# A third token tile among the first: tile 2 loaded earlier, transposed raw, and centred by a matmul

## The chip, the cores and the metric

The kernel runs on one core of a Trainium2 chip. The time is device microseconds (us) of one execution, as the median of several; a profiled execution gives the trace from which all durations here come. The engines are TensorE (PE; PEld is its weight load), VectorE (DVE), ScalarE (ACT), GpSimd (POOL) and SyncE (SP). SyncE, ScalarE and GpSimd each also issue DMAs on a queue of their own. On-chip memory is SBUF; matmuls write to PSUM, which has eight banks of 512 float32 columns by 128 partitions.

## The reference

The input x has 2048 tokens of 512 features, in bfloat16. Tokens are normalised (layer norm without weights), and two branches are added to x:

```
xn = (x - mean(x)) / sqrt(var(x) + 1e-5)
# branch A: a diagonal complex recurrence over the tokens
Lam_bar = exp(dt * Lam);  Bu = xn @ B_bar.T
h[t] = Lam_bar * h[t-1] + Bu[t]
A = 2 * real(h @ C.T) + xn * Dskip
# branch B: a gated feed-forward layer, F = 1376
B = (silu(xn @ w_gate) * (xn @ w_up)) @ w_down
out = x + A + B
```

## The kernel before, in words

The 2048 tokens are handled in four chunks of 512, each made of four tiles of 128 tokens. Tokens arrive with a token per partition, but a matmul that contracts over the 512 features needs features on partitions, so each tile has to be transposed. For chunks 1 to 3 this is done by a transposing DMA after the norm (`xT_dma`, L262). Chunk 0 would have to wait too long for that, so its first three tiles are treated differently; this is the part that the change touches.

The order of each engine's instructions is the order of the program text: the scheduler is switched off (`manual_schedule`, L64). Each engine executes its own list in order and waits by semaphores for what it reads and for the buffers that it overwrites. VectorE's work for later stages is held in a list, `backlog`, from which `pump` emits pieces between TensorE's matmuls (L623 to L649).

**Loads.** The first DMAs are listed at L125 to L143. On SyncE's queue: tile 0 of x, the first half (feature rows k = 0, 1) of the first gate group, tile 2 of x, both halves of the first up group, tile 3, then the other weights and chunk 1. On ScalarE's queue: tile 1, and the second half (k = 2, 3) of the first gate group. The weights of the gate and up matrices come in three groups of columns: two of 512 and one of 352.

**Chunk 0, tiles 0 and 1.** `raw_mm` transposes the raw tile by four matmuls against an identity (L238), each giving a 128x128 block k in PSUM. The mean is taken off inside PSUM: `sum_dve` (L221) lets VectorE sum a tile's features, and `cT_mean` (L245) adds, by a matmul of that sum, broadcast, against a matrix of -1/512 on the diagonal, the negative mean to the blocks. `raw_copy` (L249) copies the blocks to `xcT`, alternating between ScalarE and VectorE. The division by the deviation is not applied to the tokens; it is applied as the `scale` of the activation that evicts each result (`sw_scale`, L495).

**Chunk 0, tile 2** is centred by VectorE: `center` (L225) sums the tile, scales the sum to a mean, and subtracts it. Four matmuls transpose the centred tile into one bank, and ScalarE copies it out in one piece (L730 and L731).

**Chunk 0, tile 3** goes through the norm on VectorE and a transposing DMA (`xT0_dma`, L258). Tiles 0 to 2 are normalised on VectorE as well, for branch A.

**Head of the matmul stream.** `head_mm` (L693) multiplies a tile, as stationary operand, by rows of the first gate or up group, and `held` keeps a PSUM bank for each tile and matrix. Gate for tiles 0 and 1 comes first, row by row, then up rows 0 and 1, tile 2's transposes, up rows 2 and 3, then gate and up of tile 2. `sw_out` (L508) evicts a pair on ScalarE: Silu of the gate to `g0`, and a scaled copy of the up result; a product on VectorE follows. The loop at L779 does the other column groups and tile 3.

**Statistics.** `ln_stats` (L183) and `ln_stats_half` (L187) are VectorE's mean and variance; `ln_rstd` (L192) adds the epsilon on VectorE and takes the power -1/2 on GpSimd. ScalarE's evictions of a tile wait for its rstd. GpSimd also computes `dt_t`, an exponential of the parameters (`exp_pool`, L282), which arrive by `prm_transpose` (L277).

**Afterwards** come the B projections (`bproj_tile`, L380) of chunk 0, the rest of the gate/up work, and then, chunk after chunk, projections, gate/up, and the output matmuls (L599 with w_down, L612 with the recurrence's result). SyncE's queue carries the transposing DMAs in program order: chunk 0's, B's two, chunk 1's, the gate-up product of chunk 0 (`g0_dma`, L525, in two calls), then w_down, C's two, chunk 1's last gate-up block and chunk 2's tokens.

Of the kernel before, what the change touches and what calls it, by code (L numbers as in the profile page):

```python
# [10 lines left out]
F32 = mybir.dt.float32  # L11
BF16 = mybir.dt.bfloat16
ALU = mybir.AluOpType
# [10 lines left out]
def kernel(  # L24
# [17 lines left out]
    nc = tc.nc  # L42
    _, L, D = A_x.shape
# [4 lines left out]
    HW = CW // 2  # L48
# [3 lines left out]
    KD = D // 128  # L52
# [11 lines left out]
    const = ctx.enter_context(tc.tile_pool(name="const", bufs=1))  # L64
# [9 lines left out]
    def bank(shape=(128, CW), dtype=F32):  # L74
        return psum.tile(list(shape), dtype, name="ps")
# [4 lines left out]
    x_v = A_x[0].rearrange("(n p) d -> p n d", p=128)  # L80
# [5 lines left out]
    xall = const.tile([128, NT, D], BF16, name="xall")  # L86
# [30 lines left out]
    def load_w1_half(q, tiles, view, gi, k0, k1):  # L117
        a, b = fgroups[gi]
        q.dma_start(out=tiles[gi][:, k0:k1, :], in_=view[:, k0:k1, a * 128:min(F, b * 128)])

    HK = KD // 2
# [4 lines left out]
    nc.vector.memset(xall[:, 1, 0:2], 0.0)  # L126
    nc.scalar.dma_start(out=xall[:, 1, :], in_=x_v[:, 1, :])
    nc.scalar.preload_act_table_set("silu_and_others")
    load_w1_half(nc.sync, wg_g, wg_v, 0, 0, HK)
    load_w1_half(nc.scalar, wg_g, wg_v, 0, HK, KD)  # L130
    nc.sync.dma_start(out=xall[:, 2, :], in_=x_v[:, 2, :])
    load_w1_half(nc.sync, wu_g, wu_v, 0, 0, HK)
    load_w1_half(nc.sync, wu_g, wu_v, 0, HK, KD)
    nc.sync.dma_start(out=xall[:, 3, :], in_=x_v[:, 3, :])
# [45 lines left out]
    def by_k(ap):  # L180
        return ap.rearrange("p (k d) -> p k d", d=128)
# [5 lines left out]
    def ln_stats_half(n, h):  # L187
        nc.vector.bn_stats(out=stats[:, n, h, :], in_=xall[:, n, h * HW:(h + 1) * HW])
        if h == 1:
            nc.vector.bn_aggr(out=mv[:, n, :], in_=stats[:, n, :, :])  # L190
# [21 lines left out]
    xcT, xc = CF[:, 0], CF[:, 1]  # L212
    SW = TPC - 1
    def rows_first(ap):
        return flat(ap).rearrange("p (i k d) -> p k i d", k=KD, i=TPC)

    xn_c[0], xnT0 = rows_first(xc), rows_first(xnT[:, 0])
    sums = const.tile([128, 2], BF16, name="sums")
    mean = const.tile([128, 2, 2], F32, name="mean")

    def sum_dve(i, dst):  # L221
        nc.vector.scalar_tensor_tensor(out=xnT[:, NCH - 1, i, 0:HW], in0=xall[:, i, 0:HW], scalar=1.0,
                                       in1=xall[:, i, HW:D], op0=ALU.mult, op1=ALU.add, accum_out=dst)

    def center(i):  # L225
        total, m = mean[:, i - 2, 0:1], mean[:, i - 2, 1:2]
        sum_dve(i, total)
        nc.vector.tensor_scalar(out=m, in0=total, scalar1=1.0 / D, scalar2=None, op0=ALU.mult)
        nc.vector.tensor_scalar(out=xc[:, i, :], in0=xall[:, i, :], scalar1=m, scalar2=None, op0=ALU.subtract)

    p2, p0, p1 = bank(), bank(), bank()
    held = [[None, None] for _ in range(TPC)]
    held[0][0], held[1][0], held[0][1], held[1][1], held[2][0] = (bank() for _ in range(5))
    warm = held[1][0]
    raw = [[p0, p1, held[2][0], held[1][1]], [p2, held[0][1], p2, held[0][1]]]

    def cT_mm(ps, src, k, first, stop):
        nc.tensor.matmul(ps[:, k * 128:(k + 1) * 128], lhsT=src[:, k * 128:(k + 1) * 128], rhs=ident[:], start=first,  # L238
                         stop=stop)

    def raw_mm(i):
        for k in range(KD):
            cT_mm(raw[i][k], xall[:, i, :], k, all(p is not raw[i][k] for p in raw[i][:k]), False)

    def cT_mean(i, *ks):  # L245
        nc.tensor.matmul(by_k(raw[i][ks[0]][:])[:, ks[0]:ks[-1] + 1:HK], lhsT=sums[:, i:i + 1].to_broadcast([128, 128]),
                         rhs=minus_mean[:, None, :].to_broadcast([128, len(ks), 128]), start=False, stop=True)

    def raw_copy(i, k):  # L249
        cT_copy(V.tensor_copy if k % 2 else nc.scalar.copy, raw[i][k], i, k, k + 1)  # L250

    def cT_copy(copy, ps, i, k0=0, k1=KD):
        copy(out=xcT[:, k0:k1, i * 128:(i + 1) * 128], in_=by_k(ps[:, k0 * 128:k1 * 128]))
# [12 lines left out]
    lre, lim, ldt = prm[:, 0, :], prm[:, 1, :], prm[:, 2, :]  # L266

    def sm(name, *shape):
        return const.tile([128, *shape], F32, name=name)

    dt_t, r_t, dre = sm("dt_t", NQ), sm("r_t", NQ), sm("dre", NQ)
# [3 lines left out]
    V = nc.vector  # L275

    def prm_transpose():  # L277
        pp = p1[:, 0:128]
        nc.tensor.matmul(pp, lhsT=prm_rows[:], rhs=ident[:], start=True, stop=True)  # L279
        V.tensor_copy(out=prm[:].rearrange("p t q -> p (t q)"), in_=pp[:, 0:3 * NQ])  # L280

    def exp_pool(out, in_):  # L282
        nc.gpsimd.tensor_tensor(out=out, in0=e_t[:], in1=in_, op=ALU.pow)
# [205 lines left out]
    def sw_mm(ps, groups, gi, i, k0=0, k1=KD):  # L489
        a, b = fgroups[gi]  # L490
        for k in range(k0, k1):
            nc.tensor.matmul(ps[:, 0:(b - a) * 128], lhsT=tokens(i, k), rhs=groups[gi][:, k, 0:(b - a) * 128],  # L492
                             start=(k == 0), stop=(k == KD - 1))

    def sw_scale(i):  # L495
        return rstd[:, i:i + 1] if i < SW else 1.0

    def sw_gate(gi, i, psg):
        a, b = fgroups[gi]
        nc.scalar.activation(out=g0[:, a:b, i, :], in_=by_k(psg[:, 0:(b - a) * 128]), func=ACT.Silu, scale=sw_scale(i))  # L500
# [7 lines left out]
    def sw_out(gi, i, psg, psu):  # L508
        a, b = fgroups[gi]
        key, h, w = u_home(gi, i)  # L510
        if key not in u_pair:
            u_pair[key] = up_p.tile([128, 2, CW], BF16, name="u2")
        if psg is not None:
            sw_gate(gi, i, psg)
        nc.scalar.activation(out=u_pair[key][:, h, 0:w], in_=psu[:, 0:w], func=ACT.Copy, scale=sw_scale(i))
        if h == 1:
            if key[-3:] == "g01":
                g = g0[:, 0:b, i, :].rearrange("p (h f) d -> p h f d", h=2)
                u = u_pair[key][:].rearrange("p h (f d) -> p h f d", d=128)
            else:  # L520
                g = g0[:, a:b, i - 1:i + 1, :]
                u = u_pair[key][:, :, 0:w].rearrange("p i (f d) -> p f i d", d=128)
            products.append(lambda: V.tensor_tensor(out=g, in0=g, in1=u, op=ALU.mult))
# [168 lines left out]
    G, U = wg_g, wu_g  # L692
    def head_mm(which, i, k0=0, k1=KD):  # L693
        if held[i][which] is None:
            held[i][which] = bank()
        sw_mm(held[i][which], (G, U)[which], 0, i, k0, k1)
# [2 lines left out]
    dummy(warm, 5, 128)  # L699
    nc.vector.tensor_scalar(out=minus_mean[:], in0=ident[:], scalar1=-1.0 / D, scalar2=None, op0=ALU.mult)  # L700
    for i in range(2):
        sum_dve(i, sums[:, i:i + 1])
    raw_mm(0)
    for k in range(HK):
        cT_mean(0, k)
# [7 lines left out]
    for i in range(2):  # L713
        head_mm(0, i, 0, HK)
        for k in range(HK, KD):
            raw_copy(i, k)
    for k in range(HK, KD):
        for i in range(2):
            head_mm(0, i, k, k + 1)
    ln_stats_half(0, 0)  # L720
    center(2)
    ln_stats_half(0, 1)
    ln_rstd(0, 1)
    ln_stats(1)
    ln_rstd(1, 2)
    for k in range(HK):
        for i in range(2):
            head_mm(1, i, k, k + 1)
    for k in range(KD):
        cT_mm(p1, xc[:, 2, :], k, k == 0, k == KD - 1)  # L730
    cT_copy(nc.scalar.copy, p1, 2)  # L731
    for k in range(HK, KD):
        for i in range(2):
            head_mm(1, i, k, k + 1)
    ln_stats(3)
    ln_rstd(3, 4)
    head_mm(0, 2)
    sw_gate(0, 0, held[0][0])
    prm_transpose()
    ln_stats(2)  # L740
    ln_rstd(2, 3)
    exp_pool(dt_t[:], ldt)
    pad_last()
    nc.gpsimd.iota(out=jidx[:], pattern=[[1, CW]], base=0, channel_multiplier=0,
                   allow_small_or_imprecise_dtypes=True)
    sw_out(0, 0, None, held[0][1])
    head_mm(1, 2)
    norm_dve(SW)
    xT0_dma(SW, TPC)
    for n in range(SW):  # L750
# [15 lines left out]
    def sw_both(gi, i):  # L766
        cols = (fgroups[gi][1] - fgroups[gi][0]) * 128
        if 2 * cols <= CW:
            both = bank()[:, 0:2 * cols].rearrange("p (w f) -> p w f", w=2)
            for k in range(KD):  # L770
                nc.tensor.matmul(both, lhsT=tokens(i, k), rhs=w_end[:, k, :, 0:cols], start=(k == 0),  # L771
                                 stop=(k == KD - 1))
            return both[:, 0], both[:, 1]
        psg, psu = bank(), bank()
        sw_mm(psg, G, gi, i)
        sw_mm(psu, U, gi, i)
        return psg, psu

    for gi, i in [(1, 0), (1, 1), (1, 2), (2, 0), (2, 1), (2, 2), (0, 3), (1, 3), (2, 3)]:  # L779
        both = sw_both(gi, i)  # L780
        if (gi, i) == (1, 0):
            sw_out(0, 2, *held[2])
            params_sin()
        sw_out(gi, i, *both)
        pump(2 * KD * (fgroups[gi][1] - fgroups[gi][0]) * 128 / CW * 0.2163)
        multiply(1)
    multiply(0)
# [120 lines left out]
```

## Time and profile before

| what | us |
|---|---|
| median of 3 runs | 178.22 |
| lowest and highest | 178.09, 178.89 |
| the profiled execution | 178.8 |
| span of its trace | 176.7 |
| TensorE matmuls, busy | 171.1 |
| VectorE, busy | 157.3 |
| ScalarE, busy | 102.6 |
| GpSimd, busy | 28.2 |

The span runs from the first instruction of the program to the last; the rest of the profiled execution's time lies around it. A line of the timeline gives start and duration in us, the engine, the line of the kernel, the operation, and what is written from what, with the number of instructions merged into it; in brackets stand the idle time before it and what ended that. Matmuls are pipelined, so the duration of one is longer than its distance to the next. In the list of waits the columns are the total in us, the number of times, and the longest. In the list of DMA queues they are packets, MB, and the share of 16 DMA engines.

### The profile page before, as it was taken

The numbers are of one execution on the slowest core, as the hardware profiler recorded it, in microseconds if no ns is written. First come the engines' busy times: TensorE is split into PE (matmuls) and PEld (weight loads), VectorE is DVE, ScalarE is ACT, GpSimd is POOL, SyncE is SP. The second block draws the span as 40 slices with busy tenths as digits, with TensorE's granted clock in tenths as the row PEclk, the third lists the DMA queues.
The fourth block names the chain that finished last, engine by engine and source line by source line (L and its number), as shares of the span: only waits on it lengthen the run. The fifth ranks groups of instructions, "written<-read, shape, count | busy, mean of one in ns | idle before, by whom it ended". The sixth has DMA issues, their size and how long they took to land.

```text
span 176.7 us, 2366 instructions
## 1 busy us (share of the span) xinstructions
PE 171.1 (97%) x847; PEld 82.2 (47%) x863; DVE 157.3 (89%) x263; ACT 102.6 (58%) x188; POOL 28.2 (16%) x39
## 2 busy tenths in 40 slices
PE   8799999999999999999999999999999999999993
PEld 5344445564444444446444444446444444444543
DVE  3778998999999999999999999999999998699242
ACT  3186949797986687035797661014666656981000
POOL 5164300041000000046100000024100002325200
PEclk9999999999999999999999999999999999999999
DMA  5999959949999600027027000006401000994812
GB/s 153 354 346 171 172 102 220 261 95 219 238 205 244 238 0 4 0 31 81 8 48 104 0 0 0 0 0 70 52 8 24 0 4 0 127 186 64 98 59 63
DMA packets 35099, 17.88 MB, mean 101 GB/s; under 512 B 24896, under 2 KB 34976, under 8 KB 35008
## 3 DMA queue, kind: packets, MB, share of 16 engines
q1 hardware_dynamic: 31072, 13.96, 34.8%
q0 software_dynamic: 3456, 3.28, 14.9%
q10 hardware_dynamic: 560, 0.49, 1.0%
q8 instruction: 7, 0.11, 0.2%
q14 instruction: 4, 0.03, 0.1%
HBM read 8.03 MB, written 5.24 MB: 75 GB/s over the span
## 4 chain that ended last, share of the span: by engine, by line
PE 92%; DMA 5%; issue 1%; SPq 0%; DVE 0%
PE ps L460 27%; PE ps L599 21%; PE ps L385 16%; PE ps L612 16%; PE ps L492 8%; PE ps L542 3%; DMA xnT<-xn 3%; DMA wg<-in_B_w_gate_dram 2%; PE ps L771 2%; SPq L125 0%; DVE xall L615 0%; PE ps L238 0%; PE ps L279 0%
## 5 line engine op out<-in xcount | busy, mean ns | idle before, releaser
L599 PE MATMUL ps<-wd_sb,guT 128*128 128x512 bf16 (+4 forms) x184 | 38.7, 367 | 0.2
L427 DVE TENSOR_TENSOR_SCAN g<-r_t,car,u 128x512 bf16<-128x512 f32 x24 | 29.0, 1265 | 0.0
L612 PE MATMUL ps<-CF,wt 128*128 128x512 bf16 (+2 forms) x134 | 28.4, 366 | 0.1
L385 PE MATMUL ps<-xnT,BT 128*128 128x512 bf16 x125 | 28.1, 379 | 0.2
L599 PEld LDWEIGHTS <-guT 128*128 128x128 bf16 (+1 forms) x187 | 17.9, 98 | 20.5
L460 PE MATMUL ps<-xnT,wu 128*128 128x512 bf16 x95 | 24.6, 379 | 0.2
L460 PE MATMUL ps<-xnT,wg 128*128 128x512 bf16 x91 | 23.9, 379 | 0.1
L619 POOL DMA_DIRECT2D out_dram<-res x12 | 10.5, 1042 | 79.9 <-ACT res L618 74.6
L474 ACT ACTIVATE guT<-ps 128x512 bf16<-128x512 f32 x30 | 18.1, 605 | 5.1 <-PE ps L460 5.0
L475 ACT CAST u<-ps 128x512 bf16<-128x512 f32 x30 | 17.7, 589 | 5.4 <-PE ps L460 5.4
L618 ACT CAST res<-ps 128x512 bf16<-128x512 f32 x12 | 6.9, 583 | 22.7 <-PE ps L612 22.7
L387 ACT CAST u<-ps 128x512 bf16<-128x512 f32 x32 | 17.5, 616 | 4.1 <-PE ps L385 4.1
L612 PEld LDWEIGHTS <-wt 128*128 128x128 bf16 x136 | 13.0, 98 | 14.7
L385 PEld LDWEIGHTS <-BT 128*128 128x128 bf16 x128 | 12.4, 98 | 15.2 <-DMA xnT<-xn 0.5
L573 ACT ACTIVATE xr<-xall,nb,rstd 128x512 bf16<-128x512 bf16 x16 | 11.9, 805 | 7.2 <-DVE xall L581 3.6
L460 PEld LDWEIGHTS <-wu 128*128 128x128 bf16 x96 | 9.4, 98 | 11.3
L460 PEld LDWEIGHTS <-wg 128*128 128x128 bf16 x96 | 9.4, 98 | 10.6
L194 POOL TENSOR_TENSOR rstd<-ve,neg_half 128x1 f32<-128x1 f32 (+1 forms) x7 | 7.5, 1078 | 27.9 <-DVE ve L193 27.9
L460 PE MATMUL ps<-xnT,w_end 128*128 128x512 bf16 x48 | 10.9, 379 | 0.0
L479 DVE TENSOR_TENSOR guT<-guT,u 128x1024 bf16<-128x1024 bf16 x15 | 10.1, 676 | 0.0
L184 DVE BATCH_NORM_STATS2 stats<-xall 128x6 f32<-128x512 bf16 x15 | 10.1, 671 | 0.0
L395 DVE TENSOR_TENSOR pm<-u,c 128x2048 bf16<-128x2048 bf16 x8 | 9.8, 1222 | 0.1
(123 smaller groups left out, 210.5 us busy)
## 6 DMA issues: line engine op xcount, KB each, us to landing
out_dram<-res POOLq DMA_DIRECT2D x12, 128.0 KB, 3.2
out_dram<-xall POOLq DMA_DIRECT2D x3, 512.0 KB, 6.0
wd_sb<-in_B_w_down_dram SPq DMA_DIRECT2D x1, 1280.0 KB, 9.0
xall<-in_A_x_dram SPq DMA_DIRECT2D x1, 1024.0 KB, 7.2
out_dram<-in_A_x_dram SPq DMA_DIRECT2D x4, 256.0 KB, 4.8
wu<-in_B_w_up_dram SPq DMA_DIRECT2D x2, 256.0 KB, 4.9
wg<-in_B_w_gate_dram SPq DMA_DIRECT2D x1, 512.0 KB, 5.9
wu<-in_B_w_up_dram SPq DMA_DIRECT2D x1, 512.0 KB, 6.9
```

Of the source, the lines that this page charges most:

```text
L184: nc.vector.bn_stats(out=stats[:, n, 0, :], in_=xall[:, n, :])
L385: nc.tensor.matmul(ps[:] if c else by_k(ps[:]), lhsT=BT[:, part, k, q * 128:(q + 1) * 128], rhs=xnT[:, c, k, :] if c else xnT0[:, k], star ...
L387: nc.scalar.copy(out=u_tiles[c][:, part, q, :], in_=ps[:])
L427: V.tensor_tensor_scan(out=g()[:, part, q, :], data0=r_t[:, q:q + 1].to_broadcast([128, CW]), data1=u_tiles[c][:, part, q, :], initial=ini ...
L460: nc.tensor.matmul(ps[:fs, lo:hi], lhsT=wslice(groups, fi, k), rhs=xnT[:, c, k, lo:hi], start=(k == 0), stop=(k == KD - 1))
L474: nc.scalar.activation(out=guT[:fs, fi, :], in_=psg[:fs], func=ACT.Silu)
L475: nc.scalar.copy(out=u_pair[c][:fs, fi % 2, :], in_=psu[:fs])
L492: nc.tensor.matmul(ps[:, 0:(b - a) * 128], lhsT=tokens(i, k), rhs=groups[gi][:, k, 0:(b - a) * 128], start=(k == 0), stop=(k == KD - 1))
L573: nc.scalar.activation(out=box["xr"][:], in_=xall[:, n, :], func=ACT.Identity, scale=rstd[:, n:n + 1], bias=nb[:, n:n + 1])
L599: nc.tensor.matmul(o[:], lhsT=gu_tiles[c][:fsz[fi], fi, i * 128:(i + 1) * 128], rhs=wd_sb[:fsz[fi], fi, lo:hi], start=(fi == 0), stop=False)
L612: nc.tensor.matmul(o[:], lhsT=w_tiles[c][:, part, q, i * 128:(i + 1) * 128], rhs=CF[:, part, q, lo:hi], start=False, stop=(part == 1 and q ...
L619: nc.gpsimd.dma_start(out=out_v[:, n, lo:hi], in_=res[:, lo:hi], accum_op=ALU.add)
```

## The change

Five things change, all in chunk 0.

1. Tile 2 of x is issued on ScalarE's queue, second after tile 1 and ahead of the second half of the first gate group; it leaves SyncE's queue.
2. Tile 2 is transposed raw, like tiles 0 and 1, into the two banks p0 and p1 (blocks 0 and 2 in p0, 1 and 3 in p1), its mean is taken off by two matmuls of `cT_mean`, and it is copied out in two halves, one on ScalarE and one on VectorE. `center` is gone, and `sums` has three columns.
3. In the order of the matmuls, tile 2's transposes stand between the gate rows 0, 1 and the gate rows 2, 3 of tiles 0 and 1; its mean matmuls stand after row 2. Its gate matmuls follow, and then the up rows go over three tiles at a time.
4. The statistics of tiles 0, 1 and 3 stand after that copy on VectorE; `dt_t`'s power stands ahead of tile 2's rstd on GpSimd; the Silu of tile 0 is no longer issued apart from its up copy.
5. The four matmul groups of tiles 0 and 1 with the second column group (two gate, two up) are issued before the loop, into four banks taken at once; the loop uses them.

```
@@ loads
     nc.scalar.preload_act_table_set("silu_and_others")
+    nc.scalar.dma_start(out=xall[:, 2, :], in_=x_v[:, 2, :])
     load_w1_half(nc.sync, wg_g, wg_v, 0, 0, HK)
     load_w1_half(nc.scalar, wg_g, wg_v, 0, HK, KD)
-    nc.sync.dma_start(out=xall[:, 2, :], in_=x_v[:, 2, :])
     load_w1_half(nc.sync, wu_g, wu_v, 0, 0, HK)
@@ helpers
-    sums = const.tile([128, 2], BF16, name="sums")
-    mean = const.tile([128, 2, 2], F32, name="mean")
+    sums = const.tile([128, SW], BF16, name="sums")
...
-    def center(i):
-        total, m = mean[:, i - 2, 0:1], mean[:, i - 2, 1:2]
-        sum_dve(i, total)
-        nc.vector.tensor_scalar(out=m, in0=total, scalar1=1.0 / D, scalar2=None, op0=ALU.mult)
-        nc.vector.tensor_scalar(out=xc[:, i, :], in0=xall[:, i, :], scalar1=m, scalar2=None, op0=ALU.subtract)
...
-    raw = [[p0, p1, held[2][0], held[1][1]], [p2, held[0][1], p2, held[0][1]]]
+    raw = [[p0, p1, held[2][0], held[1][1]], [p2, held[0][1], p2, held[0][1]], [p0, p1, p0, p1]]
@@ head
         head_mm(0, i, 0, HK)
         for k in range(HK, KD):
             raw_copy(i, k)
+    sum_dve(2)
+    raw_mm(2)
     for k in range(HK, KD):
         for i in range(2):
             head_mm(0, i, k, k + 1)
+        if k == HK:
+            for h in range(HK):
+                cT_mean(2, h, h + HK)
+            for h in range(HK):
+                copy = V.tensor_copy if h else nc.scalar.copy
+                copy(out=xcT[:, h::HK, 2 * 128:3 * 128], in_=by_k(raw[2][h][:])[:, h::HK])
     ln_stats_half(0, 0)
-    center(2)
     ln_stats_half(0, 1)
     ln_rstd(0, 1)
     ln_stats(1)
     ln_rstd(1, 2)
-    for k in range(HK):
-        for i in range(2):
-            head_mm(1, i, k, k + 1)
-    for k in range(KD):
-        cT_mm(p1, xc[:, 2, :], k, k == 0, k == KD - 1)
-    cT_copy(nc.scalar.copy, p1, 2)
-    for k in range(HK, KD):
-        for i in range(2):
-            head_mm(1, i, k, k + 1)
     ln_stats(3)
     ln_rstd(3, 4)
     head_mm(0, 2)
-    sw_gate(0, 0, held[0][0])
-    prm_transpose()
+    for k in range(KD):
+        for i in range(SW):
+            head_mm(1, i, k, k + 1)
+        if k == HK:
+            prm_transpose()
+    exp_pool(dt_t[:], ldt)
     ln_stats(2)
     ln_rstd(2, 3)
-    exp_pool(dt_t[:], ldt)
     pad_last()
...
-    sw_out(0, 0, None, held[0][1])
-    head_mm(1, 2)
+    sw_out(0, 0, *held[0])
@@ the second column group
+    first = [[bank() for _ in range(2)] for _ in range(2)]
+    for which in range(2):
+        for i in range(2):
+            sw_mm(first[which][i], (G, U)[which], 1, i)
+    sw_out(0, 2, *held[2])
     for gi, i in [(1, 0), (1, 1), (1, 2), (2, 0), (2, 1), (2, 2), (0, 3), (1, 3), (2, 3)]:
-        both = sw_both(gi, i)
+        both = (first[0][i], first[1][i]) if gi == 1 and i < 2 else sw_both(gi, i)
+        sw_out(gi, i, *both)
         if (gi, i) == (1, 0):
-            sw_out(0, 2, *held[2])
             params_sin()
-        sw_out(gi, i, *both)
```

More of the change, by code (lines that the diff above doesn't have):

```diff
@@ L217, with sum_dve @@
     xn_c[0], xnT0 = rows_first(xc), rows_first(xnT[:, 0])
-    sums = const.tile([128, 2], BF16, name="sums")
-    mean = const.tile([128, 2, 2], F32, name="mean")
-    def sum_dve(i, dst):
+    sums = const.tile([128, SW], BF16, name="sums")
+    def sum_dve(i):
         nc.vector.scalar_tensor_tensor(out=xnT[:, NCH - 1, i, 0:HW], in0=xall[:, i, 0:HW], scalar=1.0,
-                                       in1=xall[:, i, HW:D], op0=ALU.mult, op1=ALU.add, accum_out=dst)
-    def center(i):
-        total, m = mean[:, i - 2, 0:1], mean[:, i - 2, 1:2]
-        sum_dve(i, total)
-        nc.vector.tensor_scalar(out=m, in0=total, scalar1=1.0 / D, scalar2=None, op0=ALU.mult)
-        nc.vector.tensor_scalar(out=xc[:, i, :], in0=xall[:, i, :], scalar1=m, scalar2=None, op0=ALU.subtract)
+                                       in1=xall[:, i, HW:D], op0=ALU.mult, op1=ALU.add, accum_out=sums[:, i:i + 1])
     p2, p0, p1 = bank(), bank(), bank()
@@ L701 @@
     for i in range(2):
-        sum_dve(i, sums[:, i:i + 1])
+        sum_dve(i)
     raw_mm(0)
```

## The prediction

> **What bounds the kernel now.** I read the page's totals first, then the chain that ended last, then the waits of the matmuls and of the weight loads, and then the first 14 us in order of time.
>
> ```profile
> PE 171.1 (97%) x847; PEld 82.2 (47%) x863; DVE 157.3 (89%) x263; ACT 102.6 (58%) x188; POOL 28.2 (16%) x39
> PE 92%; DMA 5%; issue 1%; SPq 0%; DVE 0%
> PE ps L492 <- DMA wg<-in_B_w_gate_dram: 1.2, 1, 1.2
> PEld L385 <- DMA xnT<-xn: 0.5, 1, 0.5
> ```
>
> TensorE is the bound, and it really waits in two places only: 1.21 us for the first gate rows, and for chunk 2's transposed tokens at 57 us. Around the first place, in order of time:
>
> ```profile
> 3.87 0.49 PE L246 MATMUL ps<-minus_mean,sums 128*128 128x128 bf16 x4
> 5.57 1.89 PE L492 MATMUL ps<-wg,CF 128*128 128x512 bf16 x8 [1.21 <-DMA wg<-in_B_w_gate_dram]
> 6.17 0.42 DVE L222 SCALAR_TENSOR_TENSOR xnT<-xall 128x256 bf16<-128x256 bf16 x1 [0.76 <-DMA xall<-in_A_x_dram]
> 7.30 1.03 PE L492 MATMUL ps<-wu,CF 128*128 128x512 bf16 x4
> 8.16 0.39 PE L238 MATMUL ps<-ident,CF 128*128 128x128 bf16 x4
> 8.38 1.03 PE L492 MATMUL ps<-wu,CF 128*128 128x512 bf16 x4
> 10.44 0.17 DVE L280 COPY prm<-ps 128x12 f32<-128x12 f32 x1 [0.48 <-PE ps L279]
> 13.49 0.16 DVE L286 TENSOR_TENSOR dre<-dt_t,prm 128x4 f32<-128x4 f32 x1 [0.59 <-POOL dt_t L283]
> ```
>
> From 5.57 on matmuls follow without a gap: eight 512-column ones from 5.57 to 7.30 are 0.216 us each, four 128-column transposes 8.16 to 8.38 are 0.055 each. So no later work on tile 2 costs a wait there today. The second place:
>
> ```profile
> 37.31 0.32 DVE L549 TENSOR_TENSOR guT<-guT,ul 128x384 bf16<-128x384 bf16 x1
> 53.38 3.62 PE L460 MATMUL ps<-xnT,w_end 128*128 128x512 bf16 x16
> 57.05 6.59 PEld L385 LDWEIGHTS <-BT 128*128 128x128 bf16 x32 [0.54 <-DMA xnT<-xn]
> ```
>
> Sixteen matmuls from 53.38 are issued by 56.84, and the next starts at 57.05: TensorE has only 0.2 us to spare. SyncE brings that transpose, in order behind the second gate-up transpose (37.70, which waits for VectorE's product at 37.31), w_down (39.03 and 40.11), both C transposes (40.99, 48.30), g_last (51.28) and then xn (52.57). From 13.49 to 37.31 VectorE has one gap, 0.73 us at 28.27, where ScalarE was itself held by VectorE's sine argument. So a late VectorE at 13.5 us is late at 37.3 and makes TensorE late at 57.
>
> **The change part by part.**
>
> *Loads.* Tile 2's DMA (L131, 128 KB) goes from SyncE's queue, behind the first gate half, to ScalarE's, ahead of the second gate half. Issues last 0.42 to 0.47: SyncE's later loads are issued about 0.47 earlier, and ScalarE issues the second gate half at 1.8 instead of 1.34. No compute is behind it: ScalarE's first copy is at 3.75. The page's q10 carried 0.49 MB, ScalarE's three transfers; q1 is SyncE's. Packets in the stretches 3.0 to 3.5 and 4.0 to 4.5 us:
>
> ```profile
> q1 hardware_dynamic: 121, 0.12, 81.8%
> q10 hardware_dynamic: 7, 0.01, 15.7%
> ...
> q10 hardware_dynamic: 98, 0.10, 66.0%
> q1 hardware_dynamic: 33, 0.03, 19.3%
> ```
>
> The queues do not share evenly: ScalarE's is nearly silent while SyncE's first gate half moves, then takes most. They alternate transfer by transfer. The order was x0, x1, gate half 0, gate half 1, x2, up half 0; it becomes x0, x1, gate half 0, x2, up half 0, gate half 1. Gate half 1 then has the 1152 KB in and ahead of it that up half 0 had, and up half 0 landed 2.16 + 4.8 = 6.98. With even sharing it would land at 1.34 + 4.4 = 5.75 plus 128 KB at half of the 362 GB/s of 5.5 to 6.0, 0.72: 6.47. I take 6.98, since the two stretches show alternation, and keep both ends. Gate half 0 keeps its place, so I leave the start at 5.57.
>
> The Trainium skill ("DMA: Bandwidth & Descriptors", Queues, rings and completion order) says that a DMA engine takes turns between queues a whole packet at a time, typically 9 to 17 descriptors. The 7 against 121 packets agree. By that rule gate half 1 lands at 6.98 and the sum is +0.8; by even sharing it would be +0.45.
>
> *Tile 2 on TensorE.* Four matmuls on half 0 end at 5.57 + 0.86 = 6.43, the four raw transposes (the four of L238, only moved) at 6.65. The next matmul waits for gate half 1 until 7.02: 0.37 lost. New are two mean matmuls of 256 columns, half of 0.216 each: +0.22. Removed is VectorE's scale and centring (0.15 + 0.35). ScalarE's 512-column copy (0.58) becomes 256 columns on ScalarE and 256 on VectorE. No row has that form: ScalarE's lie between 0.27 (128) and 0.58 (512), so 0.37; VectorE's 128-column copy takes 0.29 and its 12-column one 0.17, so 0.42 by the slope; bounds 0.29 and 0.58 for both. Tile 2's gate matmuls need ScalarE's copy: the first mean matmul ends about 0.27 after its start at 7.45, the copy at about 8.12, the weight load is ready at 8.2, and TensorE would be free at 8.10: about 0.1 more (0 to 0.3). TensorE is then 0.37 + 0.22 + 0.1 = 0.7 late.
>
> *VectorE.* It executes in order, and its new copy waits for TensorE, with all layer-norm statistics behind it. The first half-statistic, at 5.00 today, moves behind the copy. The second mean matmul ends at 7.56 + 0.27 = 7.83, the copy runs 7.89 to 8.31, two half-statistics follow, and their aggregate, 7.55 today, comes at about 9.04. The three statistics then keep their spacing (7.55 to 9.81), so the last variance is at 11.3. The parameter copy today waits 0.48 for TensorE at 10.44; both inputs now arrive at 11.35, so it moves by 0.9. On POOL the power for `dt_t` (1.15) moves ahead of tile 2's rstd (0.65): rstd of tile 3 ends about 12.1, `dt_t` 13.25, rstd of tile 2 13.93. Tile 2's norm waits for that, starts 13.97, and `dre` follows 0.345 later at 14.31 against 13.49: +0.82. That POOL's swap costs little is because `dre` waited 0.59 for `dt_t` anyway.
>
> *What the lateness meets.* The two xn transposes and B's transposes move by about 1 us on SyncE. B_re is issued at 14.85 + 1.1 and lands 6.8 later, 22.8; TensorE wants it at 23.12 + 0.7. Tile 3's transpose landed about 15.1, wanted at 18.8. Neither waits. Tile 2's Silu waits for rstd until 13.95 (12.37 today), with ScalarE's other evictions behind it; the three-tile order finishes their banks earlier than they are rewritten: tile 2's gate bank, free at 14.6, is taken again at 16.21 + 0.7, and the pre-computed group-1 banks have 2 us or more. The new four-bank prefetch adds no matmul. So TensorE stays 0.7 late until 57. There VectorE's 0.82 arrives through SyncE: TensorE's own 0.7 less the 0.2 spare is smaller, so the later decides: **+0.82**.
>
> The profiled execution took 178.8 with a span of 176.7, so 2.1 lie outside; the sum makes 179.6 there. That execution is 0.6 above the median, 178.22. Set on the median: **179.0 us**, +0.46%. I call 0.5%, 0.9 us, no change, about what a measurement tells apart here.
>
> **Rivals.**
>
> *A, the forecast:* gate half 1 late, 178.7 to 179.5 with the copies' bounds.
>
> *B, gate half 1 in time (shared queues):* no 0.37, so 0.45: 178.7. For it: landings overlap, and one engine's late end decides each landing. Against: 7 packets to 121.
>
> *C, worse: the timed runs before start earlier than the profiled one.* Before can gain until tile 2's landing binds VectorE, which had 0.48 spare at 10.44; the changed kernel cannot, since gate half 1 and not the first rows then holds it. Price 0.82 + 0.48: 179.5. For it: the 0.6 between profiled run and median. Against: profiling itself may cost that.
>
> *D, the other side: not slower.* Gate half 0 competes with a 128 KB transfer instead of 256 KB, and on the engine that finished it last it comes earlier; gate half 1 follows tile 2 directly. At best TensorE starts near 4.55 (its raw work ends 4.36), and with gate half 1 by tile 2's kind of place the third row is used at 4.55 + 1.08 = 5.63 instead of 7.02: 0.82 - 1.39 = -0.57, 177.6. It decides as soon as gate half 1 is there by 6.2 and the start is before 5.1. Against: gate half 1 landed 5.75 even without 128 KB ahead. The 0.2 spare at 57 and shorter copies could carry it to 177.3.
>
> **Chances.** A 0.48, B 0.14, C 0.25, D 0.13. A's middle lies almost on the bound at 179.1: half of A (0.25) and all of C are slower by over 0.5%: 0.50. The other half of A (0.23), B and 0.05 of D are within: 0.42. The rest of D is faster: 0.08. The range 178.1 to 180.0 takes in A, B and C with the longest copies (179.5 + 0.3 and a little), and leaves out D and the far end of C.
>
> **What the profile after would show.** Right: the landing wait of the first rows still near 1.2 us; a second wait of the gate matmuls on wg of some 0.4 us after the raw transposes; no statistics on VectorE before about 8 us; `dre` near 14.3; the weight load at L385's place near 57.9 still waiting for xn; no new PE wait on ScalarE between 11 and 30 us. If gate half 1 is there at 6.65, B holds; if the first matmul starts before 5.1, D. Wrong would be: a wait on an evicted bank in the first 30 us, VectorE's lateness not reaching 57, or a first start far from 5.57 in either direction, as it is one landing of one execution.

## The result

The changed kernel is slower: 179.76 us against 178.38 us, medians of seven runs each, a ratio of 1.0088 with a 95% interval of 1.007 to 1.0106. The forecast was 179.0, in a range of 178.1 to 180.0. The direction and the range hold; of the size, the medians' difference of 1.4 us, the forecast gave a little over half. Medians here are of all runs of a kernel; ratios and their intervals leave out single runs that lie more than 1.5% above the fastest of their kernel.

The profiled execution of the changed kernel took 179.51 us, with a span of 177.5. From its page, the busy times and the chain that ended last by engine:

```profile
PE 172.7 (97%) x849; PEld 83.2 (47%) x865; DVE 156.9 (88%) x262; ACT 102.9 (58%) x188; POOL 28.2 (16%) x39
PE 94%; DMA 3%; issue 1%; ACT 0%; DVE 0%; ACTq 0%
```

TensorE is still nearly the whole chain. The DMA in it was 5% (by the page before, 3% the tokens' transpose and 2% the first gate weights) and is 3%, all of it gate weights. The kernel did not become shorter: one wait went and another came. The waits of the matmuls (waited for, us in total, times, longest) now read:

```profile
PE ps L662 <- PEq L889: 0.8, 1, 0.8
PE ps L485 <- DMA wg<-in_B_w_gate_dram: 0.4, 1, 0.4
```

and the first microseconds of TensorE in order of time (start, duration, engine, line, operation; in brackets the idle time before it and what ended that):

```profile
4.07 0.85 PE L239 MATMUL ps<-minus_mean,sums 128*128 128x128 bf16 x4
4.71 1.91 PE L485 MATMUL ps<-wg,CF 128*128 128x512 bf16 x4
6.41 0.55 PE L231 MATMUL ps<-ident,xall 128*128 128x128 bf16 x4
7.37 0.59 PE L485 MATMUL ps<-wg,CF 128*128 128x512 bf16 x2 [0.40 <-DMA wg<-in_B_w_gate_dram]
7.80 0.38 PE L239 MATMUL ps<-minus_mean,sums 128*128 128x256 bf16 x2
```

The wait of 1.2 us ahead of the first gate matmuls is gone: they start at 4.71 instead of 5.57. The wait for the second gate half is new and sits behind tile 2's raw transposes. It shows as only 0.40 because the work ahead of it ran at half pace. The first four gate matmuls stand 0.427 us apart (1.70 from 4.71 to 6.41), where later ones stand 0.216 apart.

The same on VectorE and ScalarE, at the copy of tile 2 and where its lateness leaves:

```profile
8.10 0.37 ACT L720 CAST CF<-ps 128x256 bf16<-128x256 f32 x1 [2.76 <-PE ps L239]
8.21 0.42 DVE L720 CAST CF<-ps 128x256 bf16<-128x256 f32 x1 [2.23 <-PE ps L239]
8.55 0.74 DVE L188 BATCH_NORM_STATS2 stats<-xall 128x6 f32<-128x256 bf16 x2
14.23 0.16 DVE L279 TENSOR_TENSOR dre<-dt_t,prm 128x4 f32<-128x4 f32 x1
```

The way to 57 us, in order of time (VectorE's product, SyncE's issues, TensorE's matmuls and its weight load):

```profile
38.04 0.33 DVE L542 TENSOR_TENSOR guT<-guT,ul 128x384 bf16<-128x384 bf16 x1
...
49.37 2.05 SPq L843 DMA_TRANSPOSE CT<-in_A_C_im_dram  x1
51.59 1.19 SPq L544 DMA_TRANSPOSE guT<-g_last  x1
52.88 1.79 SPq L256 DMA_TRANSPOSE xnT<-xn  x1
...
54.41 3.62 PE L453 MATMUL ps<-xnT,w_end 128*128 128x512 bf16 x16
...
57.64 2.26 PEld L378 LDWEIGHTS <-BT 128*128 128x128 bf16 x11
...
57.86 2.32 PE L378 MATMUL ps<-xnT,BT 128*128 128x512 bf16 x10
```

The weight load there waits for nothing any more; the tokens' transpose had landed at 57.25. TensorE arrives 1.03 us later than in before's trace (54.41 against 53.38) and goes straight through, so the B projections start at 57.86 against 57.05, 0.81 later. That is the forecast's sum, by another route than the forecast's, and it is not what the medians say. From the start of these B projections to the end of the span it is 119.6 us in every one of this case's twelve traces, so what a kernel loses is settled by 57 us. The experiments ask why.

### The profile page after: what moved, and what is told of

The parts are those of the page before. It is cut to its first block, busy times and chain, and to the rows that moved or that the text cites. A ratio compares the mean times of both kernels' runs of the same rounds, so it can differ in the third digit from the quotient of the medians.

```text
span 177.5 us, 2366 instructions
## 1 busy us (share of the span) xinstructions
PE 172.7 (97%) x849; PEld 83.2 (47%) x865; DVE 156.9 (88%) x262; ACT 102.9 (58%) x188; POOL 28.2 (16%) x39
## 4 chain that ended last, share of the span: by engine, by line
PE 94%; DMA 3%; issue 1%; ACT 0%; DVE 0%; ACTq 0%
PE ps L453 29%; PE ps L592 21%; PE ps L605 16%; PE ps L378 15%; PE ps L485 7%; DMA wg<-in_B_w_gate_dram 3%; PE ps L535 3%; PE ps L764 2%; ACT L128 0%; ACTq L127 0%; DVE xall L608 0%; PE ps L272 0%; PE ps L239 0%; DVE xall L126 0%; DVE e_t L164 0%
```

## Experiments

The theories were: the moved load, with the queues taking turns (the forecast); the added work on TensorE and VectorE's lateness behind it; and, once the first runs were in, that the profiled execution of before was itself a late one.

Several readings below are of landings. They are worked out from the trace's DMA records: the time at which half of the 16 DMA engines had finished their share of a transfer, and the time at which the last had (below: the middle and the last engine). Each is the landing of one execution.

### Tile 2 behind the second gate half on the same queue

```
     nc.scalar.preload_act_table_set("silu_and_others")
-    nc.scalar.dma_start(out=xall[:, 2, :], in_=x_v[:, 2, :])
     load_w1_half(nc.sync, wg_g, wg_v, 0, 0, HK)
     load_w1_half(nc.scalar, wg_g, wg_v, 0, HK, KD)
+    nc.scalar.dma_start(out=xall[:, 2, :], in_=x_v[:, 2, :])
```

> The changed kernel, with tile 2 on ScalarE's queue third, behind the second gate half and no longer ahead of it; all else as changed. Theory 1 (the queue's turns: in the profile of the changed kernel the second gate half landed at 7.33 and TensorE resumed at 7.37, later than it could use it): the half lands near 5.8 as in the kernel before, the wait on the third gate row goes, tile 2 lands by about 6.5, and the time is 178.6 to 179.0, some 0.9 under the changed kernel. Theory 2 (the new order of matmuls and statistics, not the load, costs it): 179.5 or more, as changed. Theory 3 (half and half): near 179.2.

Measured: 179.58 us, ratio 1.0076 (1.0056 to 1.0096). The first theory's time was missed; the time is the one that the second theory names, but there is still a wait for a load. It changed its object, as the matmuls' waits show:

```profile
PE ps L231 <- DMA xall<-in_A_x_dram: 1.4, 1, 1.4
```

Tile 2, now third on ScalarE's queue, landed at 7.59 on the last engine, and its raw transposes, which stand ahead of the second gate half's matmuls on TensorE, waited for it. The second gate half, back at its old place on this queue, was there on the middle engine at 4.77, but on the last only at 6.88. With these loads and this order of matmuls, neither order on ScalarE's queue brought both early: the later one held TensorE until 7.37 in one trace and 7.64 in the other.

### The kernel before with only the load moved

```
     nc.scalar.preload_act_table_set("silu_and_others")
+    nc.scalar.dma_start(out=xall[:, 2, :], in_=x_v[:, 2, :])
     load_w1_half(nc.sync, wg_g, wg_v, 0, 0, HK)
     load_w1_half(nc.scalar, wg_g, wg_v, 0, HK, KD)
-    nc.sync.dma_start(out=xall[:, 2, :], in_=x_v[:, 2, :])
```

> The kernel before, with one line moved: tile 2 is loaded on ScalarE's queue ahead of the second gate half; no other part of the change. Theory 1: the second gate half lands near 7 or later, TensorE now waits for it after only four matmuls, 0.5 to 1.0 us, and the time is 179.0 to 179.6. Theory 2: the load alone costs nothing, 178.2 to 178.6.

Measured: 179.71 us, 1.0069 (1.0043 to 1.0096), a little above the first theory's range. One line of the change, with all compute as it was, brings most of the loss. TensorE in order of time:

```profile
4.55 1.02 PE L492 MATMUL ps<-wg,CF 128*128 128x512 bf16 x4 [0.28 <-DMA wg<-in_B_w_gate_dram]
7.52 1.02 PE L492 MATMUL ps<-wg,CF 128*128 128x512 bf16 x4 [1.95 <-DMA wg<-in_B_w_gate_dram]
```

Here the first four matmuls ran at full pace, and the whole wait for the second gate half is seen: 1.95 us, where 0.5 to 1.0 was expected.

### Tile 0's statistics ahead of tile 2's copy on VectorE

```
     raw_mm(2)
+    ln_stats_half(0, 0)
+    ln_stats_half(0, 1)
+    ln_rstd(0, 1)
```

(and the same three calls taken out behind the copy).

> The changed kernel, with tile 0's statistics and rstd put on VectorE ahead of tile 2's copy out of PSUM, where VectorE waits for TensorE, instead of behind it. It tells VectorE's lateness apart. Theory 1 (TensorE's own lateness is what reaches the end; in the changed kernel's trace the weight load at 57 us no longer waits for the transposed tokens): unchanged within 0.3, 179.5 to 180.0. The prediction's step (VectorE's 0.8 us decides at 57 us): 0.3 to 0.5 faster, about 179.3.

Measured: 179.83 us, 1.0087 (1.0062 to 1.0112), the changed kernel's own ratio. VectorE did the two half-statistics at 5.85 instead of 8.55, and the time did not move. TensorE:

```profile
4.70 1.03 PE L485 MATMUL ps<-wg,CF 128*128 128x512 bf16 x4
5.57 0.39 PE L231 MATMUL ps<-ident,xall 128*128 128x128 bf16 x4
7.85 0.59 PE L485 MATMUL ps<-wg,CF 128*128 128x512 bf16 x2 [1.90 <-DMA wg<-in_B_w_gate_dram]
```

So it gains nothing to take tile 0's statistics from behind VectorE's copy. That VectorE's lateness does not matter is not shown by it: the second gate half was complete only at 7.81 in this trace, and `dre` came at 14.67, no earlier than the changed kernel's 14.23. The trace does show what the changed kernel's profile hid: with the first gate matmuls at full pace, and the half 0.48 later, the wait is 1.90.

### The second gate half at the next turn

```
-    load_w1_half(nc.scalar, wg_g, wg_v, 0, HK, KD)
-    load_w1_half(nc.sync, wu_g, wu_v, 0, 0, HK)
+    load_w1_half(nc.sync, wg_g, wg_v, 0, HK, KD)
+    load_w1_half(nc.scalar, wu_g, wu_v, 0, 0, HK)
```

> The changed kernel with two loads exchanged: the second gate half goes on SyncE's queue right behind the first, and the first up half on ScalarE's behind tile 2. Tile 2 stays second on ScalarE's queue. If the queues take turns transfer by transfer, the second gate half is now the fifth transfer and not the sixth: it lands near 6.3, there is no wait or one under 0.2, and the time is 178.7 to 179.1. If the queues share evenly by bytes, the half lands little earlier than in the kernel before, near 6, and the time is the same; if the order of matmuls and not the load costs it, 179.5 or more.

Measured: 179.1 us, 1.006 (1.0041 to 1.0079). The half landed at 5.64 on the middle engine and 6.83 on the last, and TensorE went on at 6.87. That is half a microsecond before the changed kernel's 7.37. The time is at the upper end of the first theory's range, but the half came 0.5 later than that theory had it, and TensorE waited 0.39 where 0.2 was the most expected: the last engine is 1.2 us behind the middle one.

### The changed kernel with only the load undone

```
-    nc.scalar.dma_start(out=xall[:, 2, :], in_=x_v[:, 2, :])
     load_w1_half(nc.sync, wg_g, wg_v, 0, 0, HK)
     load_w1_half(nc.scalar, wg_g, wg_v, 0, HK, KD)
+    nc.sync.dma_start(out=xall[:, 2, :], in_=x_v[:, 2, :])
```

> The changed kernel with only the load put back: tile 2 on SyncE's queue behind the first gate half, as in the kernel before; raw transposes, mean by matmul and the new order stay. Theory 1 (the load is the cost): both gate halves land by about 5.8 and tile 2 by about 6.2, so TensorE waits at most 0.3 at tile 2's transposes; what stays is the 0.3 to 0.45 of the extra matmuls and of VectorE: 178.5 to 178.9. Theory 2 (the order costs as much as the load): 179.3 or more.

Measured: 178.57 us, 1.0016 (1.0002 to 1.003), in the first theory's range. All of the new compute (raw transposes, mean by matmul, split copy, statistics behind it, the new order of the head) together costs 0.29 us by the ratio. TensorE, without a wait for the gate rows:

```profile
4.73 1.91 PE L485 MATMUL ps<-wg,CF 128*128 128x512 bf16 x4
6.44 0.54 PE L231 MATMUL ps<-ident,xall 128*128 128x128 bf16 x4
6.82 0.59 PE L485 MATMUL ps<-wg,CF 128*128 128x512 bf16 x2
```

By the ratios, the load alone costs 0.69%, the rest alone 0.16%, and both 0.88%: the parts add up within their intervals.

### The kernel before once more, for its trace

No edit.

> The kernel before, unchanged, for a second trace: where does it start when it is not the profiled run shown? The rival C of the prediction: the first gate matmul starts earlier than 5.57, and the span is 176.0 to 176.5 instead of 176.7. If the start is 5.57 by construction (a slow last share of the first gate half): 5.4 to 5.7 again.

Measured: 178.18 us, 0.9992 (0.9974 to 1.0011); its profiled execution took 178.18 with a span of 176.1, against 178.8 and 176.7 of the one that the prediction was made from. TensorE at the start and at 57 us, and its weight load there:

```profile
4.91 1.89 PE L492 MATMUL ps<-wg,CF 128*128 128x512 bf16 x8
6.96 1.02 PE L492 MATMUL ps<-wu,CF 128*128 128x512 bf16 x4 [0.17 <-DMA wu<-in_B_w_up_dram]
...
53.05 3.62 PE L460 MATMUL ps<-xnT,w_end 128*128 128x512 bf16 x16
...
56.50 3.57 PEld L385 LDWEIGHTS <-BT 128*128 128x128 bf16 x18 [0.33 <-DMA xnT<-xn]
```

The profile shows no wait for the first gate rows. They landed at 4.86 on the last engine, where the other execution had 5.53, and the matmuls started at 4.91. Against this trace the changed kernel's B projections at 57.86 are 1.36 late, close to what the medians say (1.38).

### Both kernels without GpSimd's parameter loads

These leave out the three small loads of the recurrence's parameters and put a constant in their place. The question was whether those loads delay the last engine.

```
-    nc.gpsimd.memset(prm_rows[:], 0.0)
-    for i, v in enumerate((A_Lambda_re, A_Lambda_im, A_log_dt)):
-        nc.gpsimd.dma_start(out=prm_rows[i * NQ:(i + 1) * NQ, :], in_=v.rearrange("(q j) -> q j", j=128))
+    nc.gpsimd.memset(prm_rows[:], -0.25)
```

> The changed kernel without the three loads of the parameters on GpSimd's queue; the rows are a constant instead, so the recurrence's parameters are wrong and the rest of the work is the same. It tells whether these software DMAs make the last share of each weight half late (in the changed kernel's trace the second gate half lands on half of the DMA engines by 6.10 and on the last by 7.33). If they do: the last share comes by about 6.5, the wait on the third gate row is under 0.2 and the time 178.9 to 179.3. If they do not: as changed, 179.5 to 179.9.

> The kernel before without the same three loads, with the same constant rows: the other half of that comparison. If the software DMAs delay the last share of the first gate half: the first gate matmul starts by 4.8 and the time is 177.6 to 178.0. If not: 178.1 to 178.5.

Measured: the changed kernel 179.57 us, 1.0067 (1.0042 to 1.0091); the kernel before 178.12 us, 0.9984 (0.9968 to 1.0). In the changed kernel the second gate half's last share landed at 7.09 instead of 7.33. Between the two kernels without the loads the medians differ by 1.45 us, about as much as between the two with them (1.38), so the loads are not what makes the change slower. In the kernel before, the first gate half was complete at 4.43 and its matmuls started at 4.79, which the first reading asked for, but the time is the second reading's.

### The kernel before with an up half ahead of tile 2 on SyncE

```
+    load_w1_half(nc.sync, wu_g, wu_v, 0, 0, HK)
     nc.sync.dma_start(out=xall[:, 2, :], in_=x_v[:, 2, :])
-    load_w1_half(nc.sync, wu_g, wu_v, 0, 0, HK)
```

> The kernel before with two loads exchanged on SyncE's queue: the first up half stands right behind the first gate half, and tile 2 behind the up half. ScalarE's queue is as before: tile 1, second gate half. Nothing stands ahead of the second gate half on its own queue. If the 128 KB ahead of it on its queue is what made it late: it lands near 5.8, tile 2 near 7, TensorE waits for tile 2's centring after the up rows, 178.3 to 179.0. If what SyncE's queue has next (256 KB of up rows instead of 128 KB of tile 2) makes the last share late: the second gate half lands near 6.9 again, TensorE waits 0.5 or more for it, 179.0 to 179.6.

Measured: 178.63 us, 1.0007 (0.9982 to 1.0032), no difference that can be told, and a time that the first reading names. The second gate half, at its old place on ScalarE's queue, landed at 5.04 on the middle engine and 6.22 on the last, and TensorE waited 0.5 for it, which the second reading names. In this trace the last engine lags by 1.2 us, where 128 KB next on SyncE's queue had 0.4 and 0.6 in the two traces of before; that lag alone does not bring the loss.

### The changed kernel with tile 3 as SyncE's next transfer

```
     load_w1_half(nc.scalar, wg_g, wg_v, 0, HK, KD)
+    nc.sync.dma_start(out=xall[:, 3, :], in_=x_v[:, 3, :])
     load_w1_half(nc.sync, wu_g, wu_v, 0, 0, HK)
     load_w1_half(nc.sync, wu_g, wu_v, 0, HK, KD)
-    nc.sync.dma_start(out=xall[:, 3, :], in_=x_v[:, 3, :])
```

> The changed kernel with tile 3 (128 KB) moved forward on SyncE's queue, between the first gate half and the first up half; ScalarE's queue as changed: tile 1, tile 2, second gate half. If the queues take turns transfer by transfer, the second gate half now has 128 KB less ahead of it: it lands on half of the engines by about 5.5 and on the last by 6.3 to 6.7, the wait is under 0.3, and the time 178.7 to 179.2. If the late last share has nothing to do with what stands next on SyncE's queue: 7.0 or later again, 179.4 to 179.9.

Measured: 179.42 us, 1.0051 (1.003 to 1.0072). TensorE:

```profile
6.92 0.59 PE L485 MATMUL ps<-wg,CF 128*128 128x512 bf16 x2 [0.24 <-DMA wg<-in_B_w_gate_dram]
```

SyncE's transfer between tile 2 and the second gate half is now 128 KB instead of 256 KB, and the half landed at 5.60 and 6.87 instead of 6.10 and 7.33: half a microsecond earlier on both counts. The middle engine's landing and the wait are near what turn-taking was expected to give; the last engine's is not (6.3 to 6.7), and the time is that of the other reading, so the expectation was half missed. That the half comes earlier when SyncE's transfer is smaller speaks for turns of the queues, by one trace.

### The landings side by side

| Second gate half | middle engine, us | last engine, us | runs' ratio |
|---|---|---|---|
| before, forecast's trace | 5.34 | 5.75 | |
| before once more | 5.00 | 5.56 | 0.9992 |
| before, no parameter loads | 5.04 | 5.28 | 0.9984 |
| changed, load undone | 4.84 | 5.78 | 1.0016 |
| before, up half ahead of tile 2 on SyncE | 5.04 | 6.22 | 1.0007 |
| changed, half at next turn | 5.64 | 6.83 | 1.006 |
| changed, tile 3 next on SyncE | 5.60 | 6.87 | 1.0051 |
| before, load moved | 6.10 | 7.48 | 1.0069 |
| changed, tile 2 behind the half | 4.77 | 6.88 | 1.0076 |
| changed, no parameter loads | 6.13 | 7.09 | 1.0067 |
| changed, statistics ahead of the copy | 6.35 | 7.81 | 1.0087 |
| changed | 6.10 | 7.33 | 1.0088 |

The rows fall into two groups. Where the half was complete by 6.22, the ratio is at most 1.0016; where it came after 6.8, the ratio is above 1.005. Compute as in the kernel before and compute as changed stand in both groups. Within a group the order does not hold, and a landing is one execution's where a ratio is of several. (With tile 2 behind the half it was tile 2, at 7.59, that held TensorE.)

## Why the prediction was right or wrong

**The load: right that it makes the second gate half late, 0.35 short.** Forecast: the half would come only after the first up half, at 6.98, where the last engine had the up half in before. On the middle DMA engine the order is as forecast: first gate half 4.11, tile 2 4.40, up half 5.86, second gate half 6.10. That is 0.15 ahead of the up half in before (6.25). TensorE waits for the slowest engine, and that one was 1.23 us behind the middle one, at 7.33, where the up half had 0.73: 0.50 more, less the 0.15, is the missing 0.35. In the three traces with tile 2 on SyncE behind the first gate half and the loads otherwise in place the lag of this half was 0.4 to 0.9. The Trainium skill ("DMA: Bandwidth & Descriptors", Queues, rings and completion order) says that an engine takes turns between queues packet by packet. The middle engine's 6.10 behind 5.86, and the half microsecond that tile 3 in the up half's place brings, agree with it. It is a statement on one engine and says nothing of how far the sixteen drift apart.

That whole transfers take turns, as the forecast read its two stretches, is not shown. Summed over the sixteen engines, both queues moved side by side in the changed kernel, from 4.25 to 4.75 us and from 4.75 to 5.25 (packets, MB, share):

```profile
q1 hardware_dynamic: 90, 0.09, 65.4%
q10 hardware_dynamic: 68, 0.07, 38.9%
...
q10 hardware_dynamic: 88, 0.09, 57.2%
q1 hardware_dynamic: 84, 0.08, 49.9%
```

Engines out of step with each other could add up to the same, and the trace's packets do not name their engine. Rival B's landing, 6.47, is out: in no run with tile 2 on ScalarE's queue ahead of it was the half complete by then. Its even sharing is not out on the middle engine: 5.34 + 0.72 = 6.06 there is no farther from the measured 6.10 than the up half's 6.25. Only the run with tile 3 next speaks against it, since with even sharing the size of SyncE's transfer would not matter.

**The start stays at 5.57: wrong, and this is the step that failed.** The wait of 1.21 us in the prediction's trace was one landing of one execution. The first gate half's last share came at 5.53 there, at 4.86 in the second trace of the same kernel, and at 4.29 to 4.67 in the ten traces of the other kernels, in which its place on the queue is the same. The prediction took a sum against a late execution and then set it on the median, as if all executions started that late. This is rival C's mechanism, at a chance of 0.25 and with nearly its size (179.5 against 179.76): before gains when the first rows land early, and the changed kernel can't, since the second gate half holds it. What limited before's gain in its second trace was the landing of the up rows, though, and not VectorE as C had it.

The size comes out of the second trace of before. Its first matmul of the second gate half starts at 4.91 plus four times 0.216, 5.77; in the changed kernel at 7.37: 1.60 later. By then the changed kernel has tile 2's four transposes behind it, which before does at 7.82 and which take 0.22. It adds 0.22 for the two mean matmuls and 0.09 ahead of tile 2's gate matmuls. Before waits 0.33 ahead of the up rows (6.63 to 6.96; the line shows 0.17 of it, since a matmul's duration is longer than its distance to the next), the changed kernel doesn't. 1.60 - 0.22 + 0.22 + 0.09 - 0.33 = 1.36, which is what stands at 54.41 against 53.05 and at 57.86 against 56.50. Against the prediction's own trace the same sum has 7.37 against 6.43 and no up wait: 0.94 + 0.09 = 1.03.

So the early start is 0.33 (1.36 less 1.03) of the 0.55 by which before's two traces differ at 57 us (57.05 and 56.50). The other 0.22 is the wait for the tokens' transpose there: SyncE issued it at 51.88 in the second trace and at 52.57 in the first. And an early landing is not enough for the gain. In the trace of before without the parameter loads the gate matmuls started at 4.79 but ran in part at half pace, and the up rows started at 7.31, as late as in the prediction's trace (7.30):

```profile
4.79 2.67 PE L490 MATMUL ps<-wg,CF 128*128 128x512 bf16 x8
```

The changed kernel's 7.33 is one landing too; it was 7.81 with the statistics moved. That 1.36 meets the medians' 1.38 so closely is therefore in part luck.

**The added matmuls and copies: right.** The 256-column copies took 0.37 and 0.42, as estimated from their neighbours, and the mean matmuls 0.21 together. The work without the load was measured at 0.29 us by the ratio (0.04 to 0.53), beside 0.45 forecast for it under rival B.

**VectorE to `dre`: right in the sum, in part by luck.** Forecast 14.31, measured 14.23. VectorE's copy ran from 8.21 to 8.63, 0.32 later than forecast, and what follows it took 0.40 less. The second wait on the gate weights came as forecast too, 0.40, but out of other parts: an early start, half pace and a later landing.

**No wait on banks, on B's transposes or on tile 3: right.** Beyond the gate rows the matmuls' waits show none.

**VectorE decides at 57 us: wrong.** The late product did come through, 0.73 late (38.04). But the issues of C's two transposes took 7.64 and 2.05 instead of 7.26 and 2.81, 0.38 less, and so the tokens' transpose was issued only 0.31 later (52.88 against 52.57). It landed at 57.25, and the weight load that used to wait for it doesn't. TensorE's own lateness of 1.03, less the 0.2 that before lost at this place, is the 0.81. The forecast had said the 0.82 would arrive through SyncE; that its sum agrees with the trace is chance, one error of 0.33 on TensorE (1.03 against 0.7) and one of 0.51 on SyncE (0.31 against 0.82). The run with the statistics ahead of the copy does not test this step, since `dre` came no earlier there. What the forecast treated as a firm chain had a link, a DMA issue on SyncE, whose duration varies by nearly as much as the chain was to carry: 2.81 in the prediction's trace, and 2.03 to 2.09 in the eleven others. Both this and the start were named by the forecast as signs of its being wrong.

**Rival D, not slower,** had its start right (4.71, before 5.1) and its other condition wrong: the second gate half by 6.2.

**Open:** why the last DMA engine lags the middle one by 1.0 to 1.5 us when tile 2 is second on ScalarE's queue. Leaving out GpSimd's loads takes 0.24 from the landing. With tile 2 elsewhere the lag of this half is 1.2 and 2.1 us in the two traces that have 256 KB next on SyncE's queue (an up half ahead of tile 2; tile 2 behind the half); but with 128 KB next and tile 2 second it is 1.3. So neither is the whole, and no run isolates the rest. Nor is it shown how often the timed runs of before have the late start, the half pace or the wait at 57 us; before's two traces, and the one without the parameter loads, differ in these.

## What to carry to other kernels

A transfer that is moved ahead on one queue delays what stands behind it there, and the other queue's next transfer can come first as well: 128 KB moved cost the next half 0.8 to 1.5 us on the middle engine and 1.5 to 2.3 on the last. A wait on a first landing in one profile is a sample: before a change's price is set against it, ask what the same kernel does when that landing is early, and whether the changed kernel can still profit from it. And where a chain to a far place runs through the issue of a DMA, take its spread from several instances first; the bound engine's own lateness, added up instruction by instruction, was the surer account here.

## What the runs showed of the hardware

TensorE's pace at the start differs between executions. Matmuls stand 0.427 us apart at 512 columns and 0.107 at 128 until some moment, and 0.216 and 0.055 after it. That moment was at about 3.7 us in the prediction's trace, between 4.3 and 4.9 in the second trace of before, between 4.3 and 4.7 in the one with the statistics moved, and after 6.7 in the changed kernel's. The granted clock doesn't show it; the changed kernel's stretch from 4.0 to 6.6 us (us; busy time of PE, PEld, DVE, ACT and POOL with their instructions; granted clock, DMA share, GB/s) reads 1.00:

```profile
4.00:6.60 2.60, 2.60 (x13) 1.37 (x12) 1.20 (x6) 0.65 (x4) 0.00 (x0) 1.00 1.02 315
```

The Trainium skill ("TensorE: Matmul & The Clock Gate", Part 1: The HAM clock gate) describes such a half rate until a busy window has passed, with a window that runs freely, so that the moment varies from run to run. The spacings agree; that the rate's end varies by 3 us is wider than the 0.5 us either way which the section gives for the transition. Its use for reading: a slow start fills a wait. The second gate half's late landing reads as 0.40 us of waiting in the changed kernel's trace and as 1.90 in the trace with the statistics moved. Of the 1.50 between them the landing is 0.48 (7.33 and 7.81), and the pace is the rest; the runs take the same time. So the time at which TensorE goes on (7.37 and 7.85) is to be compared, and not the wait.

The last of the sixteen DMA engines also differs from execution to execution: the first gate half, with the same transfers ahead of it, was complete at 5.53 and 4.86 in two traces of one kernel, while its middle engine had it at 3.88 and 3.92.
